# Grouped-query attention on one core: VectorE's share of the exponentials extended to chunk 381, and chunk 1 exponentiated in two parts instead of three

## The chip, the cores and the metric

The kernel runs on one core of a Trainium2 chip. The metric is the device time of one execution in microseconds (us), the median of several. The profile's span is about 1.7 us shorter than that time.

## The reference

```python
B, Hq, Hkv, Sq, Sk, D = 16, 32, 8, 288, 512, 128      # bf16
k = jnp.repeat(k, Hq // Hkv, axis=1)
v = jnp.repeat(v, Hq // Hkv, axis=1)
scores = jnp.einsum("bhqd,bhkd->bhqk", q, k) * D ** -0.5
p = softmax(scores, axis=-1)
out = jnp.einsum("bhqk,bhkd->bhqd", p, v)
```

## The kernel before

There are 128 groups (batch x key head) of 1152 query rows and 512 keys. A group's scores, with the keys on the partitions, are 4 x 1152 columns, cut into three **chunks** of 1536 (three PSUM banks): 384 chunks, n = 0 to 383. Each chunk goes through the same steps:

- TensorE writes its scores to `ps_s[n % 2]` (`op_s`), waiting for the exponential of chunk n - 2.
- ScalarE exponentiates them to bf16 in `pt_sb` (`op_exp`).
- TensorE multiplies them with the values and a column of ones: twelve matmuls for a **block** of three row tiles (`op_pv`), two chunks later.
- VectorE takes the reciprocal of the sums and scales the block into `o_sb`: the eviction (`op_rc`, `op_ev`).

In every sixth chunk, the **shared** ones, VectorE computes the last 120 columns with a bit-trick and a polynomial. TensorE writes these scores by an extra matmul into the free end of a bank of `ps_o` (`op_sy`), so that matmul has to wait until the block that used the bank is evicted.

```python
W = 120;  EVERY = 6;  LAG = 2;  FIRST = 2;  FIRST_SHARED = 6
...
def op_sy(n):
    ...
    emit(eng, [("s_ev", n - LAG - 1)], lambda: eng.matmul(
        ps_o[:, (n - LAG) % 2, BANK - W:BANK], kt_sb[...], qt_sb[...], start=True, stop=True))
...
def op_exp(n):
    ...
    parts = [(0, CH)]
    if shared(n):
        parts = [(0, CH - W)]
    if n < FIRST or n == NS - 1:
        parts = [(x, x + BANK) for x in range(0, CH, BANK)]      # three parts of 512
    ...
def shared(n):
    return FIRST_SHARED <= n < NS - NC and (n - FIRST_SHARED) % EVERY == 0    # 6, 12, ... 378
...
# TensorE                          # VectorE, block r, with n = r + LAG
for n in range(NS):                op_rc(r)
    op_s(n)                        if shared(n):      op_y(n)
    if shared(n): op_sy(n)         if shared(n - 1):  op_yu(n-1, 1); op_yu(n-1, 2); op_yp(n-1)
    if n == 2:                     op_ev(r)
        op_kt(1, range(NJ), 1)     if shared(n):      op_yb(n); op_ym(n); op_yu(n, 0)
    if n >= LAG: op_pv(n - LAG)    if r == w0 + 1:    # 376: two reductions of the overflow check
```

The keys of groups 0 and 1 are not transposed by the DMA but by TensorE (`op_kt`), from `kd_sb`; ScalarE's queue requests the second group's when the first group's are transposed and copied:

```python
op_kd(eng, 0)
eng.activation(dum[:], ..., ACTF.Exp)
for (s, n) in need(eng, [("s_k0", 2)]):
    eng.wait_ge(s, n)
op_kd(eng, 1)
```

## Time and profile before

| | before |
|---|---|
| median time | 521.99 us (three runs, 521.93 to 522.55) |
| span of the profiled run | 520.0 us |
| TensorE matmul, busy | 510.3 us (98%) |
| ScalarE, busy | 513.3 us (99%) |
| VectorE, busy | 369.6 us (71%) |

With two engines at 98 and 99% the busy shares cannot say which one sets the pace. What can is the distance between starts, over one repetition of six chunks, of each engine's work.

### The profile page before, as it was taken

The page shows a single profiled execution, that of the slowest core. Times are in us where ns is not written, and L with a number is a line of the kernel's source. Part 1 is how long each engine was busy: PE and PEld are TensorE (multiplying, and loading weights), DVE is VectorE, ACT ScalarE, POOL GpSimd, SP SyncE. Part 2 cuts the span into 40 slices and gives each one's busy share as a digit, 9 for nine tenths or more (in the row PEclk, how much of TensorE's full clock was granted, in tenths as well). Part 3 has the DMA queues.
Part 4 walks back from the last instruction along what each step waited for, and adds up shares of the span by engine and source line. Part 5 has one row for each costly group of instructions (what it writes and reads, how often), then busy time and mean ns, then how long its engine had stood idle before and what let it go on. Part 6 is the DMA issues. An engine that isn't in the chain of part 4 may idle for free.

```text
span 520.0 us, 15243 instructions
## 1 busy us (share of the span) xinstructions
PE 510.3 (98%) x6118; PEld 394.6 (76%) x6224; DVE 369.6 (71%) x1315; ACT 513.3 (99%) x393; POOL 79.8 (15%) x135
## 2 busy tenths in 40 slices
PE   8999999999999999999999999999999999999997
PEld 5777777777777777777777777777777777777776
DVE  2767767777777677676776776767767767677776
ACT  7999999999999999999999999999999999999997
POOL 2111111111111111111111111111111111111110
PEclk9999999999999999999999999999999999999999
DMA  9999999999999998999999989999998989998212
GB/s 186 237 218 230 267 194 248 225 213 210 219 233 256 208 245 201 235 248 240 215 241 209 209 225 220 241 185 209 229 240 232 227 194 201 192 234 198 86 69 93
DMA packets 253078, 110.06 MB, mean 212 GB/s; under 512 B 219728, under 2 KB 236752, under 8 KB 253008
## 3 DMA queue, kind: packets, MB, share of 16 engines
q1 hardware_dynamic: 252720, 108.82, 97.7%
q8 instruction: 49, 0.80, 0.7%
q10 hardware_dynamic: 288, 0.26, 0.2%
q14 instruction: 21, 0.17, 0.2%
HBM read 17.04 MB, written 37.75 MB: 105 GB/s over the span
## 4 chain that ended last, share of the span: by engine, by line
ACT 98%; DMA 1%; issue 1%; DVE 0%; PE 0%
ACT pt_sb L516 97%; DMA qt_sb<-in_q_dram 1%; ACT pt_sb L511 1%; PE ps_s L439 0%; DVE o_sb L585 0%; DVE o_sb L595 0%; PE ps_s L479 0%; DVE rl_sb L575 0%; PE ps_o L669 0%; DVE bad_sb L621 0%; DVE flag_i L734 0%; DVE bad_sb L618 0%
## 5 line engine op out<-in xcount | busy, mean ns | idle before, releaser
L516 ACT ACTIVATE pt_sb<-ps_s 128x1536 bf16<-128x1536 f32 (+2 forms) x384 | 508.8, 1441 | 0.0
L479 PE MATMUL ps_o<-v_sb,pt_sb 128*128 128x129 bf16 x4584 | 322.3, 220 | 1.1
L479 PEld LDWEIGHTS ps_o<-v_sb,pt_sb 128*128 128x128 bf16 x4584 | 282.8, 98 | 49.7 <-DVE o_sb L585 14.1
L439 PE MATMUL ps_s<-qt_sb,kt_sb 128*128 128x512 bf16 (+2 forms) x1430 | 290.4, 320 | 5.0 <-DMA qt_sb<-in_q_dram 0.5
L585 DVE TENSOR_TENSOR o_sb<-ps_o,rl_sb 128x384 bf16<-128x384 f32 x382 | 211.9, 555 | 9.3 <-DVE rl_sb L575 0.5
L439 PEld LDWEIGHTS ps_s<-qt_sb,kt_sb 128*128 128x128 bf16 x1536 | 123.9, 98 | 62.3 <-issue 1.1
L575 DVE RECIPROCAL rl_sb<-ps_o 128x3 f32<-128x3 f32 x382 | 68.1, 178 | 125.5 <-PE ps_o L479 124.0
L568 POOL COPY v_sb<-vd_sb 128x512 bf16<-128x512 bf16 x128 | 78.8, 616 | 429.1 <-PE ps_o L479 408.9
L549 DVE SCALAR_TENSOR_TENSOR u_sb<-u_sb,m_sb 128x120 f32<-128x120 f32 x126 | 35.6, 283 | 2.2
L556 DVE SCALAR_TENSOR_TENSOR pt_sb<-u_sb,e_sb 128x120 bf16<-128x120 f32 x63 | 17.8, 283 | 2.2
L549 DVE SCALAR_TENSOR_TENSOR u_sb<-m_sb 128x120 f32<-128x120 f32 x63 | 17.4, 277 | 0.0
L527 DVE TENSOR_SCALAR y_sb<-ps_o 128x120 f32<-128x120 f32 x63 | 15.9, 253 | 0.0
L540 DVE TENSOR_SCALAR m_sb<-t_sb 128x120 int32<-128x120 int32 x63 | 14.1, 223 | 2.2
L540 DVE TENSOR_SCALAR e_sb<-t_sb 128x120 int32<-128x120 int32 x63 | 13.6, 216 | 0.0
L450 PE MATMUL ps_o<-qt_sb,kt_sb 128*128 128x120 bf16 x63 | 13.6, 216 | 0.0
L533 DVE TENSOR_SCALAR t_sb<-y_sb 128x120 int32<-128x120 f32 x63 | 13.4, 213 | 0.0
L450 PEld LDWEIGHTS ps_o<-qt_sb,kt_sb 128*128 128x128 bf16 x63 | 6.2, 98 | 7.4
L511 ACT ACTIVATE pt_sb<-ps_s 128x512 bf16<-128x512 f32 x6 | 3.3, 616 | 2.3 <-PE ps_s L439 2.3
L411 DVE COPY kt_sb<-ps_o 128x128 bf16<-128x128 bf16 (+2 forms) x3 | 1.0, 336 | 6.2 <-PE ps_o L404 6.1
L613 DVE TENSOR_REDUCE st_sb<-rl_sb 128x1 f32<-128x72 f32 (+1 forms) x16 | 3.5, 216 | 0.0
L611 DVE TENSOR_REDUCE st_sb<-rl_sb 128x1 f32<-128x72 f32 (+1 forms) x16 | 3.5, 216 | 0.0
L417 PE MATMUL ps_o<-const-bfloat16-1.0 128*128 128x512 bf16 (+1 forms) x6 | 2.4, 570 | 0.9 <-PEq L752 0.9
(32 smaller groups left out, 12.0 us busy)
## 6 DMA issues: line engine op xcount, KB each, us to landing
out_dram<-o_sb SPq DMA_DIRECT2D x127, 288.0 KB, 3.7
vd_sb<-in_v_dram SPq DMA_DIRECT2D x31, 512.0 KB, 5.5
qt_sb<-in_q_dram SPq DMA_TRANSPOSE x128, 4.9
kt_sb<-in_k_dram SPq DMA_TRANSPOSE x32, 5.1
vd_sb<-in_v_dram SPq DMA_DIRECT2D x1, 384.0 KB, 4.6
out_dram<-o_sb SPq DMA_DIRECT2D x3, 96.0 KB, 1.6
kd_sb<-in_k_dram ACTq DMA_DIRECT2D x2, 128.0 KB, 2.7
vd_sb<-in_v_dram SPq DMA_DIRECT2D x1, 128.0 KB, 3.3
```

Source lines behind the costliest of these rows:

```text
L439: ins = emit(eng, w_x, lambda: eng.matmul(ps_s[:, n % 2, c:c + w], kt_sb[:, sl, j, gi, :], qg[:, t * P:t * P + w], start=True, stop=True))
L450: emit(eng, [("s_ev", n - LAG - 1)], lambda: eng.matmul(ps_o[:, (n - LAG) % 2, BANK - W:BANK], kt_sb[:, (g // UG) % NSLOT, j, g % UG, :], ...
L479: ins = emit(eng, w_x, lambda: eng.matmul(outs(r)[:, t - r % NC * TPC, :], pt(g, t, j), v_sb[:, sl, gi * NJ + j, 0:DV], start=(x == 0), st ...
L516: emit(eng, waits, lambda: eng.activation(d, s, ACTF.Exp, scale=scale)).then_inc(sem["s_e"], 1)
L527: emit(eng, [("s_yb", nth(n) - NB), ("s_pv", n - LAG + 1)], lambda: eng.tensor_scalar(out=y_sb[:, b], in0=ps_o[:, (n - LAG) % 2, BANK - W: ...
L533: emit(eng, [("s_ym", 2 * (nth(n) - NB)), ("s_y", nth(n))], lambda: eng.tensor_scalar(out=t_sb[:, b], in0=y_sb[:, b], scalar1=Y_MUL, scala ...
L540: emit(eng, [("s_yp", nth(n) - NB), ("s_yb", nth(n))], lambda: eng.tensor_scalar(out=dst[:, b], in0=t_sb[:, b], scalar1=mask, scalar2=bits ...
L549: lambda: eng.scalar_tensor_tensor(out=u_sb[:, b, x], in0=src, scalar=QUARTIC[x], in1=m, op0=ALU.add, op1=ALU.mult)
L556: lambda: eng.scalar_tensor_tensor(out=pt_sb[:, n % NPT, CH - W:CH], in0=u_sb[:, b, 2], scalar=QUARTIC[3], in1=e_sb[:, b].bitcast(FP32), o ...
L568: emit(eng, waits, lambda: eng.tensor_copy(v_sb[:, sl, gi * NJ:(gi + 1) * NJ, 0:D], vd_sb[:, sl, gi].rearrange("p (j d) -> p j d", d=D))). ...
L575: emit(eng, [("s_pv", r + 1)], lambda: eng.reciprocal(rl_sb[:, TPC * r:TPC * (r + 1)].unsqueeze(2), outs(r)[:, :, D:DV])).then_inc(sem["s_ ...
L585: emit(eng, waits, lambda: eng.tensor_tensor(out=o_sb[:, g % NO, t0:t0 + TPC, :], in0=outs(r)[:, :, 0:D], in1=rl_sb[:, TPC * r:TPC * (r + ...
```

## The change

The intent is to take 120 columns off one more exponential near the end, and to save one instruction's fixed cost near the start.

```diff
-    FIRST_SHARED = 6
+    PARTS = {0: (1, 2, 3), 1: (2, 3), NG * NC - 1: (1, 2, 3)}
+    SHARED = list(range(2 * NC, NS - NC, EVERY)) + [NS - NC]      # 6, 12, ... 378, and 381
...
-            if n < FIRST or n == NS - 1:
-                parts = [(x, x + BANK) for x in range(0, CH, BANK)]
+            if n in PARTS:
+                parts = [(x * BANK, y * BANK) for (x, y) in zip((0,) + PARTS[n], PARTS[n])]
...
         def shared(n):
-            return FIRST_SHARED <= n < NS - NC and (n - FIRST_SHARED) % EVERY == 0
+            return n in SHARED
```

More of the change, by code (lines that the diff above doesn't have):

```diff
@@ L372, in used, with part, ahead @@
             return max(b for b in range(NC) for t in range(b * TPC, (b + 1) * TPC) for j in range(NJ) if place(t, j)[0] == i)
+        def part(n, x):
+            return sum(x >= e for e in PARTS.get(n, (TPC,)))
+        def ahead(n):
+            return sum(len(PARTS[m]) - 1 for m in range(n))
         def ready(n, x):
-            if n < FIRST and x < TPC - 1:
-                return ("s_eb", n * (TPC - 1) + x + 1)
-            return ("s_e", n + 1 + (x if n == NS - 1 else 0))
+            p = part(n, x)
+            if n < FIRST and p < len(PARTS[n]) - 1:
+                return ("s_eb", ahead(n) + p + 1)
+            return ("s_e", n + 1 + (p if n == NS - 1 else 0))
         def sequence(b):
@@ L440, in op_s @@
                     ps_s[:, n % 2, c:c + w], kt_sb[:, sl, j, gi, :], qg[:, t * P:t * P + w], start=True, stop=True))
-                if n < FIRST and (c + w) % BANK == 0 and c + w < CH:
+                if n < FIRST and (c + w) % BANK == 0 and (c + w) // BANK in PARTS[n][:-1]:
                     ins.then_inc(sem["s_s0"], 1)
@@ L507, in op_exp @@
                 parts = [(0, CH - W)]
-            if n < FIRST or n == NS - 1:
-                parts = [(x, x + BANK) for x in range(0, CH, BANK)]
+            if n in PARTS:
+                parts = [(x * BANK, y * BANK) for (x, y) in zip((0,) + PARTS[n], PARTS[n])]
             for x, (c, e) in enumerate(parts[:-1]):
-                ins = emit(eng, [("s_s0", (TPC - 1) * n + x + 1)] if n < FIRST else waits, lambda: eng.activation(
+                ins = emit(eng, [("s_s0", ahead(n) + x + 1)] if n < FIRST else waits, lambda: eng.activation(
                     d[:, c:e], s[:, c:e], ACTF.Exp, scale=scale))
@@ L519, in shared @@
         def shared(n):
-            return FIRST_SHARED <= n < NS - NC and (n - FIRST_SHARED) % EVERY == 0
+            return n in SHARED
         def nth(n):
-            return (n - FIRST_SHARED) // EVERY + 1
+            return SHARED.index(n) + 1
         def op_y(n):
```

## The prediction

> **What bounds the kernel now.** I started with the clock (granted at 1.000 throughout, so nothing is lost there) and then the page: busy times, costliest groups.
>
> ```profile
> PE 510.3 (98%) x6118; PEld 394.6 (76%) x6224; DVE 369.6 (71%) x1315; ACT 513.3 (99%) x393; POOL 79.8 (15%) x135
> ...
> L516 ACT ACTIVATE pt_sb<-ps_s 128x1536 bf16<-128x1536 f32 (+2 forms) x384 | 508.8, 1441 | 0.0
> L479 PE MATMUL ps_o<-v_sb,pt_sb 128*128 128x129 bf16 x4584 | 322.3, 220 | 1.1
> ```
>
> ScalarE at 99% and no idle time before its exponentials looks like the bound, and the chain that ended last says the same, 97% of it L516. But TensorE is at 98%, and each record's length includes its drain, which the next record overlaps. So I read paces, start to start, from the chain in order of time (columns: start, us, what):
>
> ```profile
> 6.13 0.49 ACT pt_sb L516
> 6.62 0.98 ACT pt_sb L511 x2
> 7.60 5.61 ACT pt_sb L516 x5
> 13.26 7.97 ACT pt_sb L516 x6
> 21.28 7.93 ACT pt_sb L516 x6
> 29.26 7.93 ACT pt_sb L516 x6
> ```
>
> Every sixth chunk is shared, so the program repeats every six chunks: 21.28 to 29.26 is 7.98 us. What would ScalarE need alone? In narrow windows of the timeline the 512-wide parts of chunk 1 start at 6.50, 6.97 and 7.45 (0.477 us apart), and the whole chunks 2 and 3 start at 7.93 and 9.26 (1.331 us). The difference, 0.854 us for 1024 columns, is 0.834 ns a column; what is left of 1.331 is 0.05 us per instruction. A shared exponential (1416 columns) therefore needs 1.231, and six chunks 5 x 1.331 + 1.231 = 7.886 us. ScalarE is 0.1 us short of the period: it waits, although the page's idle column hides it. Now TensorE over the same stretch:
>
> ```profile
> 22.39 0.84 PE L479 MATMUL ps_o<-v_sb,pt_sb 128*128 128x129 bf16 x12
> 23.07 0.82 PE L439 MATMUL ps_s<-qt_sb,kt_sb 128*128 128x512 bf16 x5
> 23.72 0.84 PE L479 MATMUL ps_o<-v_sb,pt_sb 128*128 128x129 bf16 x12
> 24.40 0.38 PE L439 MATMUL ps_s<-qt_sb,kt_sb 128*128 128x512 bf16 x1
> ```
>
> Twelve value matmuls take 0.68 us (22.39 to 23.07), a chunk's score matmuls 0.65 (23.07 to 23.72): 1.33 a chunk, 7.98 for six, exactly the period, with no gap. So from about 14 us until the tail **TensorE's issue rate is the bound**, and ScalarE trails it. An exponential that is shortened in the middle would gain nothing; this change touches only the first and last few microseconds, where other rules hold.
>
> **What the Trainium skill says.** "TensorE: Matmul & The Clock Gate", section "Wait — 56ns, not 53.3ns?": start to start, N / 2.4 GHz plus about 2.5 ns once warm, N / 1.2 GHz cold; 215.7 and 426.7 ns at 512. The trace agrees: 0.65 us for three warm, and 5.23 to 5.66 cold. "ScalarE: Activation LUTs", section "What ACT_TABLE_LOAD costs": 186 ns + 0.833 ns a column for an ACTIVATE, back-to-back ones overlapping by about 93 ns. The slope agrees (0.834), but the constant left is 93 there and 50 ns here; I use 50. "Perfetto Trace Analysis", section "Per-instruction lifecycle": semaphore waits fall outside a recorded window[...]. "PSUM — Partial Sum Buffer", section "PSUM bank collisions raise a hardware error": guard PSUM with semaphores by bank. That bears on the extra score matmul below, which shares a bank of ps_o with an eviction; no run shows a collision.
>
> **Part 1: chunk 1 in two parts.** Exponentials of 512+512+512 become 1024+512: one instruction constant less, 3 x 0.477 = 1.431 becomes 0.904 + 0.477 = 1.381, so **0.05 us** off. Price: the first part must wait for two score banks.
>
> ```profile
> 5.66 0.57 PE L439 MATMUL ps_s<-qt_sb,kt_sb 128*128 128x512 bf16 x1
> ```
> ```profile
> 6.07 0.38 PE L439 MATMUL ps_s<-qt_sb,kt_sb 128*128 128x512 bf16 x1
> ```
> ```profile
> 6.02 0.60 ACT L516 ACTIVATE pt_sb<-ps_s 128x512 bf16<-128x512 f32 x1
> 6.50 0.62 ACT L511 ACTIVATE pt_sb<-ps_s 128x512 bf16<-128x512 f32 x1
> ```
>
> These are chunk 1's first two score matmuls and, on ScalarE, chunk 0's last part and chunk 1's first. Bank two is written at 6.07 + 0.38 = 6.45; a semaphore takes 0.02 to 0.04 us (ScalarE's first exponential starts 0.02 us after the matmul before it ends, in the chain). So 6.47 to 6.49, just before 6.50, when ScalarE comes free: the wait should be hidden, with almost nothing to spare. The value matmuls of chunk 0 want bank one of chunk 1 only at about 8.05; the merged part ends near 7.54. Does the 0.05 us pass on? TensorE is not saturated yet there:
>
> ```profile
> 8.96 0.94 PE L479 MATMUL ps_o<-v_sb,pt_sb 128*128 128x129 bf16 x12
> ```
>
> 0.94 against the usual 0.84: these twelve stop for chunk 2's exponential (7.93 + 1.51 = 9.44), and there is a stall of 0.03 us at 13.5 for chunk 5's. The path runs through ScalarE until then, so I take the full 0.05 us: TensorE enters its saturated stretch that much earlier.
>
> **Part 2: VectorE's share in chunk 381.** It takes 120 columns off an exponential (0.1 us of ScalarE), replaces one 512-wide score matmul by a 392-wide and a 120-wide (one more constant, some 3 ns), and adds eight VectorE instructions: by the rows of the page 253 + 213 + 223 + 216 + 277 + 283 + 283 + 283 = 2.03 us. ScalarE's 0.1 us is mostly worth nothing, as chunks 382 and 383 wait for TensorE's scores. After a shared chunk the next exponential starts about 0.02 us after its scores; three chunks later it trails them by about 0.045. Chunks 382 and 383 can therefore start **0.02 to 0.025 us** nearer to TensorE. That is the gain in the tail. There is also a price:
>
> ```profile
> 511.16 0.28 DVE L556 SCALAR_TENSOR_TENSOR pt_sb<-u_sb,e_sb 128x120 bf16<-128x120 f32 x1
> 511.34 0.81 PE L439 MATMUL ps_s<-qt_sb,kt_sb 128*128 128x512 bf16 x2
> 511.36 0.55 DVE L585 TENSOR_TENSOR o_sb<-ps_o,rl_sb 128x384 bf16<-128x384 f32 x1
> ...
> 511.96 0.69 PEld L479 LDWEIGHTS ps_o<-v_sb,pt_sb 128*128 128x128 bf16 x12 [0.31 <-DVE o_sb L585]
> 511.98 0.84 PE L479 MATMUL ps_o<-v_sb,pt_sb 128*128 128x129 bf16 x12
> ```
>
> At 511.34 TensorE issues chunk 381's scores; VectorE's eviction of block 377 (511.36) is late, because chunk 378's polynomial went first, and ends at 511.91. The value matmuls behind it just make it (511.98). Every other shared chunk is six after the last; 381 is only three after 378. Its extra matmul writes into the bank that this eviction frees and is due at 511.34 + 2 x 0.216 + 0.166 = 511.94, or 511.89 with the 0.05 us of part 1, while its weight load is released at about 511.96, or 511.91. A stall of about **0.045 us** follows, and it eats nearly all of part 1, since TensorE is saturated up to here.
>
> VectorE's late queue: after a shared chunk the next eviction ends 0.85 us late, the one after 0.19 late, then it has caught up. Here that is block 380 at 515.8, block 381 at 516.5; the reciprocal of block 382 is due at 516.47 and can start about 0.09 us before the eviction in front of it ends. It just fits. The polynomial's result (about 515.36, from the 1.19 us that it takes after its value matmuls at 15.27) is wanted at 515.67. Both fit.
>
> **Sum.** TensorE before chunk 381: -0.05. At its extra matmul: +0.045 and 0.003. Tail: -0.02 to -0.025. In all about **-0.02 to -0.03 us** of 521.99, and without the stall -0.07. I predict 521.95.
>
> **Rivals.** (a) ScalarE is the real bound: 0.05 + 0.1 = 0.15 us come off, 521.84. For it speaks the 99%; against it six chunks taking 7.98 where 7.886 would do. (b) The merged part of chunk 1 waits: the bank comes with 0.01 to 0.03 us to spare, and the clock is being released just there (the matmuls go from 0.43 apart to 0.22 at 6.07). If that came one matmul later, bank two would be ready about 0.2 us later, the gain would turn into a loss of up to 0.2 us: 522.1. (c) VectorE becomes the tail's bound: if its queue slips by more than some 0.06 us, everything after block 382 slips with it, up to +0.3: 522.3. Speaking against it is the catch-up seen after every earlier shared chunk; for it, two shared chunks so close together. (d) Input transfers land differently: the first scores wait for qt_sb until 4.4 us, and a shift there moves the whole run, in either kernel.
>
> **Range and chances.** Effects lie between -0.15 and +0.3 us, under 0.06%. Three runs of before spread over 0.62 us (521.93 to 522.55), more than any of this, so the range is that spread with some margin: 521.5 to 522.5. Two per cent would be 10.4 us; no rival has 4% of that, so the chance of no change at 2% is 0.99.
>
> **What the changed trace would show.** Part 1: a 1024-wide exponential at 6.50 without a gap, chunk 2's at 7.88 in place of 7.93, the middle repeating every 7.98 us, all 0.05 earlier. Part 2: 64 groups of 1416 wide; a weight load of L450 near 511.9 waiting for o_sb L585; chunk 382's exponential only some 0.02 earlier than 513.53; the last reciprocals not later than 516.47 and 517.16. Wrong would be a six-chunk period other than 7.98 (then the bound is not TensorE), a wait of ScalarE before 6.5, or a DVE row that holds up the last value blocks.

## The result, and the profile after

| | before | after |
|---|---|---|
| median time, same chip | 521.99 us (five runs, 521.85 to 522.75) | 522.10 us (five runs, 522.06 to 522.66) |
| ratio | | 1.0001, 95% interval 0.9986 to 1.0016 |
| span of the profiled run | 520.0 us | 521.0 us |

The time is the same within what the runs can tell, and lies in the predicted range. The first question is why the profiled run of after has a span 1.0 us longer. The page of after (busy us, share, instructions):

```profile
PE 510.9 (98%) x6119; PEld 394.9 (76%) x6225; DVE 370.9 (71%) x1323; ACT 513.5 (99%) x392; POOL 79.4 (15%) x135
```

One ScalarE instruction fewer and eight VectorE ones more, as the diff says; nothing here is 1 us. It is in the first ten microseconds of the chain of waits of after (start, us, what):

```profile
0.82 4.02 DMA qt_sb<-in_q_dram
4.89 3.71 PE ps_s L449 x12
```

(Line numbers of after are ten higher than those of before: L414 are the key transposes, L449 the scores, L489 the value matmuls, L526 and L521 the exponentials, L595 the eviction.) The first scores could start, once the queries were there, at 4.89 us and not at 4.41, and the twelve score matmuls of the first three chunks took until 8.60, still 0.43 us apart up to 7.85 us because the matmul clock was low until about 8.1 (in the trace of before it rose at about 6.0). So the transposes of the second group's keys started at 8.44 against 7.31 (before, then after):

```profile
7.31 0.40 PE L404 MATMUL ps_o<-ident,kd_sb 128*128 128x128 bf16 x4
```
```profile
8.44 0.39 PE L414 MATMUL ps_o<-ident,kd_sb 128*128 128x128 bf16 x4
```

The keys had landed at 7.86, so in this run it was the queries and the clock that held TensorE. The further traces had to show whether any of it had to do with the change. (The summary of the chain of waits is no help in telling the bound: it gives ScalarE 98% in before and TensorE 97% in after, while both repeat every 7.98 us.) A second trace of the changed kernel (experiment e5 below) had the clock up earlier; its timeline at the start is (start, us, engine, line, operation):

```profile
6.50 1.05 ACT L521 ACTIVATE pt_sb<-ps_s 128x1024 bf16<-128x1024 f32 x1
...
7.45 0.40 PE L414 MATMUL ps_o<-ident,kd_sb 128*128 128x128 bf16 x4 [0.33 <-DMA kd_sb<-in_k_dram]
...
8.45 0.81 PE L449 MATMUL ps_s<-qt_sb,kt_sb 128*128 128x512 bf16 x3
...
9.10 0.84 PE L489 MATMUL ps_o<-v_sb,pt_sb 128*128 128x129 bf16 x12
```
```profile
7.88 1.50 ACT L526 ACTIVATE pt_sb<-ps_s 128x1536 bf16<-128x1536 f32 x1
```

The merged part starts at 6.50 without a wait and chunk 2's exponential at 7.88 in place of 7.93: to the hundredth as predicted, in part because the first scores started at 4.41 in both traces. Counted from the first scores, chunk 2's exponential starts after 3.525 us with three parts (before, e3, e12) and after 3.47 with two (e5, e6, e8, e13); where the clock was up before the first scores, after 3.31 with three (e2) and 3.25 with two (e1). So part 1 does take 0.05 us off at this point, in every trace with the clock up. But now TensorE waits for the keys (until 7.45), and chunk 3's scores follow from that. The twelve value matmuls at 9.10 take 0.84 us, not 0.94: nothing waits for the earlier exponential.

At the other end, the timeline of after around chunk 381's extra score matmul:

```profile
512.96 0.10 PEld L460 LDWEIGHTS ps_o<-qt_sb,kt_sb 128*128 128x128 bf16 x1 [0.32 <-DVE o_sb L595]
512.96 0.23 PE L460 MATMUL ps_o<-qt_sb,kt_sb 128*128 128x120 bf16 x1
```

The weight load waits for the late eviction. In the trace the matmul starts 0.203 us after the 392-wide one ahead of it, where 0.166 is usual, and the first value matmul 0.062 after that, where 0.053 is usual: a stall of 0.046 us, where 0.045 was predicted.

### The profile page after: what moved, and what is told of

Its sections match the earlier page's. It is cut to its first block, busy times and chain, and to the rows that moved or that the text cites. A ratio compares the mean times of both kernels' runs of the same rounds, so it can differ in the third digit from the quotient of the medians.

```text
span 521.0 us, 15254 instructions
## 1 busy us (share of the span) xinstructions
PE 510.9 (98%) x6119; PEld 394.9 (76%) x6225; DVE 370.9 (71%) x1323; ACT 513.5 (99%) x392; POOL 79.4 (15%) x135
## 4 chain that ended last, share of the span: by engine, by line
PE 97%; issue 1%; DVE 1%; DMA 1%
PE ps_o L489 50%; PE ps_s L449 46%; DMA qt_sb<-in_q_dram 1%; PE ps_o L460 1%; DVE o_sb L595 0%; DVE u_sb L559 0%; DVE rl_sb L585 0%; DVE o_sb L605 0%; DVE pt_sb L566 0%; PE ps_o L679 0%; PE ps_o L414 0%; DVE t_sb L543 0%; DVE m_sb L550 0%; DVE bad_sb L631 0%; DVE flag_i L744 0%
## 5 line engine op out<-in xcount | busy, mean ns | idle before, releaser
L526 ACT ACTIVATE pt_sb<-ps_s 128x1536 bf16<-128x1536 f32 (+2 forms) x384 | 508.9, 1440 | 0.2 <-PE ps_s L449 0.2
L489 PE MATMUL ps_o<-v_sb,pt_sb 128*128 128x129 bf16 x4584 | 322.2, 220 | 1.1
L489 PEld LDWEIGHTS ps_o<-v_sb,pt_sb 128*128 128x128 bf16 x4584 | 282.8, 98 | 49.3 <-DVE o_sb L595 13.8
L449 PE MATMUL ps_s<-qt_sb,kt_sb 128*128 128x512 bf16 (+2 forms) x1430 | 291.2, 321 | 5.5 <-DMA qt_sb<-in_q_dram 1.0
L595 DVE TENSOR_TENSOR o_sb<-ps_o,rl_sb 128x384 bf16<-128x384 f32 x382 | 211.9, 555 | 9.2 <-DVE rl_sb L585 0.5
L449 PEld LDWEIGHTS ps_s<-qt_sb,kt_sb 128*128 128x128 bf16 x1536 | 124.1, 98 | 63.4 <-issue 2.1
L521 ACT ACTIVATE pt_sb<-ps_s 128x512 bf16<-128x512 f32 (+1 forms) x5 | 3.2, 681 | 2.9 <-PE ps_s L449 2.8
```

Of the source, the lines that this page charges most:

```text
L449: ins = emit(eng, w_x, lambda: eng.matmul(ps_s[:, n % 2, c:c + w], kt_sb[:, sl, j, gi, :], qg[:, t * P:t * P + w], start=True, stop=True))
L489: ins = emit(eng, w_x, lambda: eng.matmul(outs(r)[:, t - r % NC * TPC, :], pt(g, t, j), v_sb[:, sl, gi * NJ + j, 0:DV], start=(x == 0), st ...
L526: emit(eng, waits, lambda: eng.activation(d, s, ACTF.Exp, scale=scale)).then_inc(sem["s_e"], 1)
L595: emit(eng, waits, lambda: eng.tensor_tensor(out=o_sb[:, g % NO, t0:t0 + TPC, :], in0=outs(r)[:, :, 0:D], in1=rl_sb[:, TPC * r:TPC * (r + ...
```

## The experiments

The spread between runs of one kernel (0.2 to 1.5 us) is larger than any effect of the change. So, besides times, I use two distances in the trace that do not depend on the start: from **chunk 60's scores** (the semaphore that their last matmul raises) to the end of the last VectorE reduction, and from the start of the **key transposes** of group 1 to chunk 60's scores. Equal programs agree in them to about 0.01 us, with one exception: in e9 the clock stayed low until 10.4 us, and its distance from the key transposes to chunk 60 is 0.055 us longer.

| kernel | median us | before, same rounds | ratio (95%) | keys transposed at | keys to chunk 60 | chunk 60 to end |
|---|---|---|---|---|---|---|
| before (first trace) | 521.99 | | | 7.31 | 77.740 | 433.522 |
| after | 522.10 | 521.99 | 1.0001 (0.9986 to 1.0016) | 8.44 | 77.599 | 433.535 |
| e1, part 1 alone | 522.62 | 521.78 | 1.0015 (1.0002 to 1.0029) | 7.94 | 77.609 | 433.525 |
| e2, part 2 alone | 521.86 | 521.78 | 1.0003 (0.9990 to 1.0017) | 7.64 | 77.608 | 433.535 |
| e5, after again | 521.72 | 521.79 | 0.9994 (0.9981 to 1.0007) | 7.45 | 77.610 | 433.532 |
| e6, part 1 again | 522.14 | 521.79 | 1.0005 (0.9992 to 1.0019) | 7.56 | 77.611 | 433.523 |
| e8, check earlier | 521.77 | 521.79 | 0.9995 (0.9982 to 1.0008) | 7.49 | 77.611 | 433.487 |
| e9, keys at once | 523.67 | 521.79 | 1.0031 (1.0018 to 1.0045) | 10.31 | 77.665 | 433.535 |
| e11, keys at 3.2 us | 522.24 | 521.99 | 1.0002 (0.9989 to 1.0016) | 8.77 | 77.609 | 433.487 |
| e12, e11 with three parts | 521.96 | 521.99 | 1.0006 (0.9992 to 1.0019) | 7.22 | 77.817 | 433.487 |
| e13, more dummy matmuls | 521.96 | 521.99 | 0.9999 (0.9986 to 1.0013) | 9.27 | 77.609 | 433.486 |

**e1: part 1 alone** (the share in chunk 381 taken out again).

```diff
-    SHARED = list(range(2 * NC, NS - NC, EVERY)) + [NS - NC]
+    SHARED = list(range(2 * NC, NS - NC, EVERY))
```

> Part 1 alone: chunk 1 in two parts, no share in chunk 381. My theory: if the matmul clock is released by about 6.1 us, chunk 2's exponential starts about 0.05 us earlier and the whole run is 0.05 us shorter than before; if the clock is still low until 7.7 us (as in the trace of after), chunk 2's exponential waits for its scores anyway and the change is worth 0.00. Median 521.9 to 522.0. Rival (the merged part waits for its second bank and delays the run): 0.1 to 0.25 us longer than before in runs of the same kind.

Measured: 521.69 to 523.16 us, median 0.84 above before. In its trace chunk 2's exponential starts early, as it should (3.25 us after the first scores, against 3.31 in e2 below), but the keys come at 7.94, 0.99 us after TensorE has run out of work. By the trace the change cost nothing, but the five times looked bad enough to repeat (e6).

**e2: part 2 alone** (chunk 1 in three parts again).

```diff
-    PARTS = {0: (1, 2, 3), 1: (2, 3), NG * NC - 1: (1, 2, 3)}
+    PARTS = {0: (1, 2, 3), 1: (1, 2, 3), NG * NC - 1: (1, 2, 3)}
```

> Part 2 alone: share in chunk 381, chunk 1 in three parts. My theory: the weight load of the extra score matmul of chunk 381 waits for the late eviction, TensorE stands 0.045 us, the tail wins back 0.02 us: 0.02 to 0.03 us longer than before. Rival (ScalarE is the bound): 0.1 us shorter. Rival (VectorE's late queue is the bound of the tail): over 0.1 us longer, with the last reciprocals waiting behind an eviction.

Measured: median 0.08 us above before, within noise. From chunk 60 to the end 433.535 us against 433.522: part 2 costs 0.013 us. TensorE's stall is there again, 0.048 us, so the tail gives back 0.035. ScalarE's 0.1 us did not come off, and VectorE did not become the bound: the last two points of that expectation are refuted.

**e3: no shared chunk at all** in the kernel before, to ask what the pace of the middle is.

```diff
-    FIRST_SHARED = 6
+    FIRST_SHARED = 1000
```

> The kernel before with no shared chunk at all: ScalarE exponentiates all 384 chunks whole. If TensorE's issue rate is the bound (1.330 us a chunk against 1.331 for a whole exponential): 522.0 to 522.6. If ScalarE is the bound: 63 x 0.1 us longer, 528.3.

Measured: 527.57 us, ratio 1.0109 (1.0094 to 1.0125). My theory missed this. The chain of waits of e3, in its repeating part:

```profile
17.29 43.02 ACT pt_sb L516 x32
```

43.02 us for 32 whole exponentials is 1.344 us each, not the 1.331 that I had read. The reason can be seen in the trace of before, in narrow windows of ScalarE's timeline (chunks 2, 3 and 4):

```profile
7.93 1.51 ACT L516 ACTIVATE pt_sb<-ps_s 128x1536 bf16<-128x1536 f32 x1
...
9.26 1.52 ACT L516 ACTIVATE pt_sb<-ps_s 128x1536 bf16<-128x1536 f32 x1
...
10.59 1.53 ACT L516 ACTIVATE pt_sb<-ps_s 128x1536 bf16<-128x1536 f32 x1
```

The starts are 1.331 apart, but each record is about 0.012 us longer than the one before: the starts run ahead of the ends. From end to end (9.437, 10.780, 12.124 in the trace) it is 1.343 to 1.344. In the middle of e3 (chunks 198 to 211), too, the ends are 1.343 to 1.345 apart, while the starts lie 1.335 to 1.350 apart. A start-to-start distance over a few instructions behind a pause is too short, by exactly what the records grow.

**e4: one value matmul in twelve left out**, a wrong result (relative error 0.32), to lighten TensorE by 0.057 us of 1.330 a chunk.

```diff
             todo = sequence(r % NC)
+            del todo[1]
```

> Wrong result on purpose: the kernel before with one of the twelve value matmuls of each block left out (0.057 us of 1.330). If TensorE is the bound: the period of six chunks falls from 7.98 to ScalarE's 7.89, so 62 x 0.097 = 6.0 us shorter, about 516.0. If ScalarE is the bound: no change.

Measured: 520.94 us, ratio 0.9979 (0.9964 to 0.9994): about 1 us, not 6.0. The chain of waits of e4:

```profile
22.35 2.60 ACT pt_sb L517 x2
...
30.31 2.60 ACT pt_sb L517 x2
```

The period of six chunks is 7.96 us. With ScalarE's pace corrected that is what it needs alone: five whole exponentials at 1.344 and one shared, 0.100 shorter, 7.964. So before stood at 7.98, TensorE's need, and ScalarE's was only 0.02 below it.

**e10: both at once**, no shared chunk and one value matmul in twelve left out (wrong, too). After e3 a rival was left: that a loop of waits (one exponential, then the value matmuls that need it, then the next scores) sets the unshared kernel's pace, rather than ScalarE's own rate. Worked out from the trace of e3 that loop is 4.03 us per three chunks, the same number.

> Wrong result on purpose: no shared chunk and one value matmul in twelve left out. Theory now: ScalarE's own pace is 1.344 us a whole exponential, read from end to end (the records lengthen by 12 ns each while the starts are 1.331 apart), so it alone sets this kernel: the same as with no shared chunk, about 527.5 us, period of six chunks 8.06. Rival (a loop of waits through one exponential and the matmuls of two blocks sets the unshared kernel's pace): the loop is 0.057 us per three chunks shorter, 522 to 523 us.

Measured: 527.07 us, ratio 1.0095 (1.0079 to 1.0110). The chain of waits of e10:

```profile
22.61 2.64 ACT pt_sb L517 x2
...
30.66 2.65 ACT pt_sb L517 x2
```

8.05 us for six chunks, so 4.03 for three, unchanged with TensorE lightened. TensorE only stands idle for longer: 0.21 us per three chunks near chunk 200, against 0.04 in e3. The loop would have shortened, so this rival falls, and ScalarE's pace of 1.344 stands. The four kernels together:

| | all twelve value matmuls | eleven |
|---|---|---|
| every sixth chunk shared | 521.8 to 522.0 (before) | 520.9 (e4) |
| none shared | 527.6 (e3) | 527.1 (e10) |

Sharing is worth 5.8 us and brings ScalarE just below TensorE; after that, lightening TensorE alone is worth about 1 us. (ScalarE lightened further in the middle was not tried; that TensorE's matmuls leave no gap there says that it would give nothing.)

**e5: the changed kernel again**, and **e6: part 1 alone again**, unchanged files, on another chip.

> The changed kernel again, for more of its times and a second trace. Theory now (from five traces): the run is the start of the second group's key transposes plus a fixed 510.9 to 511.0 us, and what differs between runs is when those keys land and when the matmul clock is released, not the change; then the times mix with those of before (median within 0.3 us of it), and from chunk 60's scores to the end it takes 433.53 us. Rival (part 1 costs something in most runs, as the ten runs with it, median 522.3, against nineteen without, median 521.9, could say): median again 0.3 us or more above before.

> Part 1 alone again, for the same question. Theory (luck of the start): within 0.3 us of before. Rival (part 1 costs something): again 0.5 us or more above before, and the trace shows where, before chunk 4's scores.

Measured: e5 521.72 us (521.57 to 521.86), 0.07 below before; e6 522.14 (521.64 to 523.10 in six runs), 0.35 above, with an interval that includes no difference. The full change, which contains part 1, shows no cost; e1 and e6 scatter more. In both traces everything after the key transposes is as in the other kernels: 77.61 and 433.53 or 433.52, together 511.14 us (the expectation's 510.9 to 511.0 was added up wrongly). So no trace shows a cost of part 1 in the program. What the scattered runs had in common I cannot show, since only one run of each has a trace. Also open: with the request at the same place in the program, the second group's keys took 2.99 to 3.31 us to land in the traces with three parts (before, e2, e3, e4, e10), and 3.12 to 3.60 in those with two (after, e1, e5, e6, e8), 4.76 in e13. The two overlap; with one trace of each run I make nothing of it.

**e8: the overflow check's two reductions one block earlier**, out of the way of the late eviction.

```diff
                 if r == w0:
                     op_stat(B - 1)
-                if r == w0 + 1:
+                if r == w0:
                     emit(eng, [("s_stat", B)], lambda: eng.tensor_reduce(
```

> The changed kernel, with the two small reductions of the overflow check moved from block 376, ahead of the late eviction of block 377, to block 375, where VectorE has room. Theory: block 377's eviction ends 0.09 us earlier, the extra score matmul of chunk 381 no longer waits (stall 0.045 us to 0.00), and from chunk 60's scores to the end it takes 433.49 in place of 433.535 us. Rival (the stall is only the shape of the instructions): unchanged at 433.53. The median cannot show it (spread of starts is 0.5 us).

The timeline of e8 at the extra matmul:

```profile
511.93 0.10 PEld L460 LDWEIGHTS ps_o<-qt_sb,kt_sb 128*128 128x128 bf16 x1 [0.22 <-DVE o_sb L595]
...
511.99 0.22 PE L460 MATMUL ps_o<-qt_sb,kt_sb 128*128 128x120 bf16 x1
```

The weight load still waits for the eviction, but starts 0.06 us before its matmul is due, and no matmul is late (0.166 and 0.052 us after the one ahead, the usual distances); from chunk 60 to the end it takes 433.487 us against 433.532 in e5: 0.045 us back, as expected. In the median (521.77) this cannot be seen.

**e9: the second group's keys requested at once.** Since their landing set the start in most traces, I asked for them earlier.

```diff
             op_kd(eng, 0)
+            op_kd(eng, 1)
             eng.activation(dum[:], ...)
-            for (s, n) in need(eng, [("s_k0", 2)]):
-                eng.wait_ge(s, n)
-            op_kd(eng, 1)
```

> The changed kernel, with the second group's keys requested at once after the first group's (0.9 us in place of 4.3). Theory (the landing of these keys and the clock set the start): the key transposes follow the first scores without a wait at about 6.9 to 7.3 us if the clock is up, the chain of waits no longer holds the keys, and the median falls by 0.2 to 0.6 us, unless the earlier request delays the queries by as much. Rival (the start is bound by ScalarE or by the clock): no change.

Measured: 523.67 us, ratio 1.0031 (1.0018 to 1.0045). The hoped-for gain did not come; what the expectation named as an exception did, and by more. The chain of waits of e9:

```profile
0.82 5.62 DMA qt_sb<-in_q_dram
...
6.49 4.02 PE ps_s L449 x12
```

The first queries, behind the keys, arrive 2.1 us later than in before. In this trace the clock also stayed low until 10.4 us, so that the twelve score matmuls took 4.02 us (2.91 in before). The late request in the kernel before is there for a reason.

**e11 and e12: the keys requested when the first group's have landed** (about 3.2 us), with two parts and with three, both on top of e8.

```diff
-            for (s, n) in need(eng, [("s_k0", 2)]):
+            for (s, n) in need(eng, [("s_kd0", 16)]):
                 eng.wait_ge(s, n)
             op_kd(eng, 1)
```

> The changed kernel with the check's reductions moved, and the second group's keys requested when the first group's have landed (about 3.2 us), not when they are transposed and copied (4.3). Theory (their landing sets the start in most runs): the key transposes come at about 6.7 to 7.3 us when the clock is up early, chunk 60's scores by about 85.0, the median 0.05 to 0.2 us lower and the spread smaller. Rival (they take the place of the queries again, as when requested at 0.9): the first scores late, the median higher.

> The same, with chunk 1 in three parts again. Theory: where the keys come early the path of the start runs through ScalarE, and one part more costs 0.05 to 0.06 us: chunk 60's scores that much later than in the two-part kernel, if both traces have the keys before 7.3 us and the clock up. If they land later: no difference between the two.

Measured: 522.24 (521.53 to 522.97) and 521.96 us (521.52 to 522.82), no better than before; the earlier request does not make the keys come reliably earlier (they landed at 8.72 in e11 and at 7.17 in e12, at 7.26 in before). As a test of the 0.05 us the pair is inconclusive, as the two-part kernel's profiled run had the clock low and its keys at 8.77. But e12's trace is the one with the earliest keys, 7.22, and three parts:

```profile
8.87 1.01 PE L489 MATMUL ps_o<-v_sb,pt_sb 128*128 128x129 bf16 x12
9.48 0.23 PEld L489 LDWEIGHTS ps_o<-v_sb,pt_sb 128*128 128x128 bf16 x4 [0.17 <-ACT pt_sb L526]
```

Here TensorE does wait for chunk 2's exponential, and from the keys to chunk 60's scores it takes 77.82 us in place of 77.61. Chunk 60's scores come at 85.035 us, as in before (85.046, keys at 7.31); counted from the first scores it is 80.64 us in both. With three parts, ScalarE lets them come no sooner. Taking 77.61 off, keys before about 7.43 us (first scores at 4.40) are what it takes for part 1 to be worth anything. No trace with two parts had them so early, so that the 0.05 us then reaches the end of the run is not shown.

**e13: six dummy matmuls in place of one** while TensorE waits for the first queries, on top of e8, to have the clock up earlier.

```diff
-            op_warm(1, P, ps_s[:, 1])
+            op_warm(6, P, ps_s[:, 1])
```

> The changed kernel with the check's reductions moved, and six dummy matmuls in place of one while TensorE waits for the first queries (0.5 us more of work in its gap). Theory: the clock is released by 7.7 us at the latest, the runs of 522.4 and more become rare; median 521.5 to 521.8. Rival (the late runs are only the landing of keys): the spread stays as before, 521.6 to 522.8.

Measured: four runs within 521.78 to 521.97 us and one of 523.46, the profiled one. The chain of waits in that trace:

```profile
4.46 4.76 DMA kd_sb<-in_k_dram
```

The clock was up by 5.9 us (by 5.5 in e8 and 5.6 in e5, without the extra matmuls); these keys took 4.8 us to land, against 3.0 in before. So the rival is right at least for this run: a late run can be the landing of keys alone. Whether the other four are close together because of the dummy matmuls, four runs do not say.

No version beat before by more than the runs' spread. e8 is the best in the part that the program controls, by 0.035 us over before and 0.045 to 0.048 over the traces of after.

## Why the prediction was right or wrong

The time (522.10 us, later 521.72 against 521.79) lies in the range, and "no change within 2%" holds by far. By its steps:

- **"TensorE's issue rate is the bound, and ScalarE trails it"**: held for the kernel before: the period of 7.98 us is the one at which its matmuls follow one another without a gap, and lightening TensorE shortens it (e4). But the number beside it was wrong. "ScalarE is 0.1 us short of the period" rested on 1.331 us a chunk; e3, e4 and e10 showed 1.344, so 0.02. The step that failed is taking the pace from start to start over the first two chunks after a pause. It made the expectations of e3 and e4 miss by 5 us each, and it returns in part 2's tail below. What hides ScalarE's short wait from the page's idle column is that records overlap: after a shared chunk a record lasts 1.451 us and the next starts 1.347 after it.
- **Part 1, "0.05 us off" with the second bank just in time**: the size held (7.88 against 7.93), and so did the bank when the clock was up (6.50 without a wait). When the clock was low, as in the first trace of after, the merged part did wait, 0.26 us, as rival (b) feared; but chunk 2's scores were ready only at 8.615, as ScalarE came free (their exponential starts at 8.642, 0.477 after the one before it), so the wait cost less than 0.01 us. A clock that rises just after 6.1 us, the case that rival (b) worked out, is in no trace.
- **"The path runs through ScalarE until then, so I take the full 0.05 us"**: this step failed. It was read from one trace, in which the keys had come early; there it held. In the traces of after, e1, e5, e6 and e8 TensorE's second group of keys or its clock held chunk 3's scores: with two parts as with three (e2) it takes 77.60 to 77.61 us from the key transposes to chunk 60's scores, and part 1 was worth nothing.
- **Part 2, a stall of 0.045 us and a tail gain of 0.02 to 0.025**: the stall measured 0.046 to 0.048 (after, e5, e2), and e8 showed its cause. The lines beside the forecast give only 0.02, though (a weight load at 511.96 for a matmul due at 511.94); how 0.045 came from them is not said, so the close agreement proves little. With 0.013 us left over (e2) the tail gave back 0.035, because here, too, the gain was read at starts: without the stall (e8, counted from chunk 60's scores) chunk 382's exponential starts 0.021 us earlier than in before, as forecast, but its record is 0.016 shorter and it ends 0.037 earlier. In all part 2 costs 0.013 us where I had 0.023 to 0.028.
- **VectorE's queue "just fits"**: in after the reciprocal of block 382 still starts 0.02 us after its value matmuls, and its wait of 0.17 us from before is used up. Rival (c) fell. Rival (a) fell with e2.
- **The sum, -0.02 to -0.03 us**: from the traces it is about +0.013 where the keys or the clock set the start. So the forecast change had the wrong sign. The range was set by the spread of the runs (rival (d)), and that was the part of the prediction that carried the result; no median can tell -0.03 from +0.01 us.

## What to carry to other kernels

Read an engine's pace from end to end over a long stretch: starts behind a pause run ahead, and the sign is records that grow by the same few nanoseconds each. Before counting a gain at the start of a kernel, look at several traces for what the next engine waits for there; one trace shows one outcome of a race between transfers, clock and engines. When two engines are within a fraction of a per cent of each other, shortening the slower one is worth only that difference (here 0.02 us of 7.98, about 1 us in all).

## What the Trainium skill lacked or had wrong

- "ScalarE: Activation LUTs", section "What ACT_TABLE_LOAD costs": 186 ns + 0.833 ns a column with about 93 ns of overlap gives, as an estimate, 1.373 us for 1536 columns; measured 1.344 from end to end (e3, 32 in a row). The 512-wide parts of chunk 0 and 1 end 0.489 apart where the same sum gives 0.520. So the fixed part is 63 ns here, not 93; that section does not say whether its operands lie in PSUM, as the scores do here. The page does not say that starts can lie closer (1.331) while the records grow by 12 ns each.
- "Perfetto Trace Analysis", section "Identifying the Most-Contended Engine": it picks the engine with the highest occupancy (and would judge TensorE by other measures than its busy share). Here ScalarE reads 99% in before and in e3, though sharing changed the time by 5.8 us and in before TensorE (98%) sets the period, by 0.02 of 7.98 us. The page has no word on records that grow in length as a sign of an engine that lags.
- "TensorE: Matmul & The Clock Gate", section "Part 1: The HAM clock gate": that the release varies from run to run agrees with these traces, but by more than the ±500 ns that it gives for back-to-back matmuls: full rate from about 4 us in e1 and e2, 6 in before, 8 in after and e11, 9.5 in e10. It puts the cost of the ramp below 1% of a typical span, and that agrees: the key transposes start at 8.44 us (after) against 7.45 (e5), in the same kernel, of which 0.49 is queries that came later, so about 0.5 us of 521 is left for the clock.
- No page that I used has a figure for how small transfers delay each other: 128 KB of keys requested about 3 us earlier held the first queries back by 2.1 us (e9), and the same request took 3.0 us to land in before and 4.8 in e13.
